# One load for the last values, wo's last piece cut 5/2/1, two issues and two copies moved, in a gated decode step

## The chip, the cores and the metric

One NeuronCore of a Trainium2 chip runs the whole program. The metric is the time of one execution on the device in microseconds (us), as the median of several runs. The profile is one further execution, recorded by the hardware profiler. Its engines: PE (TensorE, matrix multiply), PEld (TensorE's weight loads), DVE (VectorE), ACT (ScalarE), POOL (GpSimd) and SP (SyncE, which here only issues DMAs). "q" behind an engine's name (SPq, PEq) is its sequencer.

## What is computed

Attention of one new token over a cache, and a feed-forward block, mixed by a gate. B = 2 sequences, D = 640, 32 heads of 128, 4096 cached keys and values for each head and sequence, F = 1728, all float32:

```python
q = (x @ wq).reshape(B, 1, 32, 128).transpose(0, 2, 1, 3)
p = softmax(einsum("bhqd,bhkd->bhqk", q, k_cache) * 128**-0.5)
o = einsum("bhqk,bhkd->bhqd", p, v_cache)
a = o.transpose(0, 2, 1, 3).reshape(B, 1, 4096) @ wo
b = silu(x @ w1) @ w2
g = sigmoid((x * gate_w).sum(-1, keepdims=True))
out = g * a + (1 - g) * b
```

The caches are 268 MB of the 298 MB that one execution reads.

## The kernel before

The 64 pairs of head and sequence are taken in 16 items of four heads of one sequence (`items`, N = 16). An item needs 8 MB of keys and 8 MB of values. SBUF holds three slabs of 8 MB: `a` and `b` take the keys of even and odd items, `v` takes values. Item 15 is the exception: its keys are in `b`, and its values go to `a`, which is free by then.

For an item i, DVE and POOL multiply the keys with the query in place (`products`), DVE sums them (`scores`) and finds the peak, ACT makes the exponentials `pz` (`weights`), PE multiplies `pz` with the values in 64 matmuls (`values`, line 734), DVE scales and masks the product (`combine`, line 766), PE folds it with one small product (`gather`, line 782, two matmul instructions), and DVE turns the row into the columns of a stationary operand `oP` (`turn`). PE runs items 0 to 14 in a hardware loop. Item 15 is written out behind the loop.

The weights of the output projection, wo, are 32 rows for each partition, 8 rows for each of four groups (`PR` = 8, `NP` = 4). Groups 0 to 2 land in slab `v` when the values of item 14 are used up; group 3 lands in slab `b`. `project(g)` (accumulate at line 558) multiplies `oP[g]` with the 8 rows of a group. Rows of groups 0 to 2 go to the half of a PSUM bank called `early`, 24 rows of four matmul instructions of 320 columns. Rows of group 3 go to the half called `acc`, 8 rows of eight instructions of 160 columns, in four stripes. `merge` joins the two: ACT copies `early` to SBUF (line 571), then PE adds it to `acc` in eight instructions (line 576). The feed-forward product lies in two further stripes of `early`, which ACT copies long before (line 621). At the end DVE copies `acc` (line 865) and SP stores it.

In the kernel before, the values of item 15 come in three loads of a half, a quarter and a quarter of a slab, and `values(15)` is three operations on PE, each waiting for its own load. Group 3 of wo comes in loads of 4, 3 and 1 rows.

The order on an engine is the order in which the program lists its operations. Each operation waits for the writers of what it reads and for the writers and readers of what it writes (`Flow.op`). A tile's name is the unit: both halves of the PSUM bank bear the name `ps_acc`, and for tiles in PSUM a reader also waits for readers on other engines. DMAs issued by SP run in the order of issue, spread over 16 DMA engines.

At the start SP issues wq (8 MB in slab `a`, 2 MB in `v`), w1 and w2, 19 MB in all, and ACT issues x and the gate's weights, 7.5 KB. PE turns x with the identity matrix (line 386), DVE prepares the gate, PE sums it (line 408), and then comes `mm_qr` (line 433) for the queries. The load of the first keys waits for the first 64 matmuls of `mm_qr`, that of the first values for the product with w1 (line 502), that of the second keys for the feed-forward product (line 607).

Of the kernel before, what the change touches and what calls it, by code (L numbers as in the profile page):

```python
# [142 lines left out]
def gated_decode(nc, x, kc, vc, wq, wo, w1, w2, gate, out):  # L143
    P = 128
    B, H, SK, DH = kc.shape
    D = x.shape[2]
# [6 lines left out]
    NG = C // 4  # L153
# [4 lines left out]
    SLAB = C * DH  # L158
# [5 lines left out]
    W2 = D // 2  # L164
    NP = HQ // 2
    PR = 2 * Q
    items = [(hq, b) for hq in range(HQ) for b in range(B)]
    N = len(items)
    LOOPED = N - 1
# [2 lines left out]
    f = Flow(nc)  # L172
    V, S_, T_, G_ = nc.vector, nc.scalar, nc.tensor, nc.gpsimd

    def sb(name, shape, align=32):
        return nc.alloc_sbuf_tensor(name, shape, F32, align_bytes=align)[tuple([slice(None)] * len(shape))]

    def bank(name):
        return nc.alloc_psum_tensor(name, [P, 512], F32)[:, :]
# [3 lines left out]
    slab = {n: sb(f"slab_{n}", [P, SLAB], 512) for n in "abv"}  # L183

    def part(n, *ks):
        return [f"{n}.{k}" for k in (ks or range(8))]
# [12 lines left out]
    pz = sb("pz", [P, NG, 32])  # L199
    g = sb("g", [P, B])  # L200
# [16 lines left out]
    row = sb("row", [64, DH])  # L217
    oP = [sb(f"oP{i}", [P, PR, 32]) for i in range(NP)]
    oE = sb("oE", [64, PR])
    side = sb("side", [P, 2])  # L220
    partial = sb("partial", [P, W2])
# [3 lines left out]
    ps_q, ps_o, ps_v, ps_acc, ps_t, ps_m, ps_0, ps_1 = (bank(f"ps{i}") for i in range(8))  # L225
    oT = ps_m[:64, 256:512].rearrange("p (n r) -> p n r", r=32)
    early, acc = ps_acc[:, :W2], ps_acc[:, W2 : W2 + W]

    h_q, h_e, h_v, h_o = (f.sem(n) for n in ("next_q", "weights", "values", "rows"))
# [6 lines left out]
    HD = D // 2  # L236
    PD = PR * D

# [6 lines left out]
    def run_of(flat, i):  # L245
        hq, b = items[i]
        return flat[b, hq].rearrange("(p c) -> p c", p=P)
# [7 lines left out]
    def load_v(i):  # L255
        src = run_of(vflat, i)
        if i < N - 1:
            v_load[i] = f.dma("SP", slab["v"], src, writes=part("v"), signal=h_v if i < LOOPED else None)
            return
        cuts = (0, SLAB // 2, 3 * SLAB // 4, SLAB)  # L260
        after = f.users(part("a"))
        for k, (c0, c1) in enumerate(zip(cuts, cuts[1:])):
            f.dma("SP", slab["a"][:, c0:c1], src[:, c0:c1], writes=part("a", k), after=after)

    def load_wo(g):

        n, at = ("v", g * PD) if g < NP - 1 else ("b", 0)
        src = wo[g * PR * P : (g + 1) * PR * P, :].rearrange("(p n) d -> p (n d)", n=PR)
        cuts = (0, PD) if g < NP - 2 else (0, PD // 2, PD) if g < NP - 1 else (0, PD // 2, PD - D, PD)
        after = f.users(part(n)) if g in (0, NP - 1) else wo_after  # L270
        for k, (c0, c1) in enumerate(zip(cuts, cuts[1:])):
            f.dma("SP", slab[n][:, at + c0 : at + c1], src[:, c0:c1], writes=part(n, g % (NP - 1) + k), after=after)
        return after
# [3 lines left out]
    wq_rows = wq.rearrange("(p j) n -> p (j n)", j=J)  # L277
    f.dma("SP", slab["a"], wq_rows[:, :SLAB], writes=part("a"))
    xg = slab["v"][: B + 1, XG_AT : XG_AT + D]
    f.dma("ACT", xg[:B], x.rearrange("b s d -> (b s) d"), writes=part("v", 6))  # L280
    f.dma("ACT", xg[B : B + 1], gate[None, :], writes=part("v", 7))
    f.dma("SP", slab["v"][:, :W1_AT], wq_rows[:, SLAB:], writes=part("v", 0))
    f.dma(
        "SP",
# [2 lines left out]
        writes=part("v", 1, 2, 3, 4, 5),  # L287
# [5 lines left out]
        writes=part("b"),  # L293
# [8 lines left out]
        reads=["ident"],  # L302
        writes=["ident"],
# [9 lines left out]
    for q in range(Q):  # L313
# [3 lines left out]
            writes=["fold"] if q == 0 else [f"fold{q}"],  # L317
# [5 lines left out]
        reads=["ident"],  # L323
        writes=["sel"],
# [4 lines left out]
        reads=["ident"],  # L329
        writes=["half"],  # L330
# [9 lines left out]
        reads=["sel"],  # L340
        writes=["pick"],
# [4 lines left out]
        reads=["sel"],  # L346
        writes=["own"],
# [4 lines left out]
        reads=["ident"],  # L352
        writes=["side"],
    )
    for q in range(Q):
# [5 lines left out]
            reads=["ident"],  # L361
            writes=[f"spread{q}"],
# [3 lines left out]
    for e in range(2):  # L366
# [5 lines left out]
            reads=["ident", "join"],  # L372
            writes=["join"],
# [4 lines left out]
            reads=["ident", "join"],  # L378
            writes=["join"],
# [18 lines left out]
    for b in range(B):  # L398
# [3 lines left out]
            reads=["ps_v", "xz"],  # L402
            writes=[f"gx{b}"],
# [5 lines left out]
        reads=["ones", "gp"],  # L409
        writes=["ps_o"],  # L410
# [7 lines left out]
        reads=["g"],  # L418
        writes=["gc"],
# [59 lines left out]
    for u in range(2):  # L479
# [9 lines left out]
            reads=["ident", f"qall{u}0"],  # L489
            writes=[f"ps_{u}"],  # L490
# [26 lines left out]
    for e in range(2):  # L517
# [3 lines left out]
            reads=["ps_v"],  # L521
            writes=[f"spaced{e}"],
# [8 lines left out]
        reads=["he", "gc"],  # L531
        writes=["he"],
    )
    for e in range(2):
# [5 lines left out]
            reads=["he", "turned", "half"],  # L540
            writes=[f"seq{e}"],
        )

    load_v(0)

    count = {"early": 0, "late": 0}
    total_of = {"early": PR * (NP - 1), "late": PR + 1}

# [16 lines left out]
        f.op("PE", fn, reads=lkeys + wkeys, writes=["ps_acc"])  # L567
        count[to] += 1

    def merge():  # L570
        f.op("ACT", lambda: S_.copy(partial[:64], early[:64, :]), reads=["ps_acc"], writes=["partial"])  # L571

        def fn():
            for n in range(G):
                e, c = divmod(n * W, W2)
                last = T_.matmul(  # L576
                    acc[32 * n : 32 * n + HB + 1, :],
                    join[:, e, :],
                    partial[:, c : c + W],
                    start=False,  # L580
                    stop=False,
                )
            return last

        f.op("PE", fn, reads=["partial", "partial2", "partial3", "join"], writes=["ps_acc"])
        count["late"] += 1

    def project(g):
        n, at = ("v", g * PD) if g < NP - 1 else ("b", 0)
        w = slab[n][:, at : at + PD]  # L590
        to = "early" if g < NP - 1 else "late"
        for k in range(PR):
            lhsT = oP[g][:, k, :] if count[to] == 0 else oP[g][:, k, : HB + 1]
            key = g if g < NP - 2 else g % (NP - 1) + (k >= PR // 2) + (g == NP - 1 and k == PR - 1)
            accumulate(lhsT, w[:, k * D : (k + 1) * D], [f"oP{g}{u}{b}" for u in range(2) for b in range(B)], part(n, key), to)
            if count["late"] == 1:
                merge()

    def ffn_out(n):

        def fn():
            for k in range(FH):
                to = 64 + 32 * (k % 2)
                last = T_.matmul(  # L607
                    early[to : to + 2 * B, :],
                    seq[:, k : k + 2, :].rearrange("p k b -> p (k b)"),
                    slab[n][:, k * HD : (k + 1) * HD],  # L610
                    start=(k < 2),
                    stop=(k >= FH - 2),
                )
            return last

        f.op("PE", fn, reads=["seq0", "seq1"] + part(n), writes=["ps_acc"])
        for k in range(2):
            to = 64 + 32 * k
            f.op(
                "ACT",  # L620
                lambda to=to: S_.copy(partial[to : to + 2 * B], early[to : to + 2 * B, :]),
                reads=["ps_acc"],
                writes=[f"partial{2 + k}"],
            )

    ffn_out("b")
    load_k(1)

# [99 lines left out]
    def values(i, by=(), loop=None):  # L728
        v = slab["v" if i < N - 1 else "a"].rearrange("p (g c) -> p g c", g=NG)

        def groups(g0, g1):
            for gr in range(g0, g1):
                q = gr % 4
                last = T_.matmul(  # L734
                    ps_v[32 * q : 32 * q + 32, :],
                    pz[:, gr, :],
                    v[:, gr, :],
                    start=(gr < 4),
                    stop=(gr >= NG - 4),
                )  # L740
            return last

        if i < N - 1:
            f.op(
                "PE",
                lambda *_: groups(0, NG),
                reads=part("v") + ["pz"],
                writes=["ps_v"],
                by=by,
                loop=loop,  # L750
                lower=[(h_v, 16)],
            )
            return
        cuts = (0, NG // 2, 3 * NG // 4, NG)
        for k, (g0, g1) in enumerate(zip(cuts, cuts[1:])):
            f.op(
                "PE",
                lambda g0=g0, g1=g1: groups(g0, g1),
                reads=part("a", k) + ["pz"],
                writes=["ps_v"],  # L760
            )

    def combine(i):
        ops["combine", i] = f.op(
# [64 lines left out]
    for i in range(N + 1):  # L829
        j = i - 1  # L830
        loop = j if 0 <= j < LOOPED else None
# [10 lines left out]
        if 1 <= i < N:  # L842
            load_v(i)
# [8 lines left out]
        if i == N - 1:  # L852
            wo_after = None
            for g_ in range(NP):
                wo_after = load_wo(g_)
# [7 lines left out]
    for g_ in range(NP):  # L863
        project(g_)
# [56 lines left out]
```

## Time and profile before

| | us |
|---|---|
| median of 3 runs | 696.61 (696.37 to 696.76) |
| the profiled execution | 696.48 |
| its span | 695.2 |
| DVE busy | 489.3 |
| POOL busy | 266.1 |
| PE busy | 224.5 |
| ACT busy | 40.7 |

The span is the time from the first to the last recorded instruction; 1.28 us of the execution lie around it. Busy time is an average over stages, so the tables of shares don't say what sets the end. For that one reads the DMA queues, then the chain that ended last, and then PE's own timeline behind its loop, where the order of its queue can be seen. The granted clock (PEclk) is given as a share of the full 2.4 GHz: 0.50 is 1.2 GHz.

### The profile page before, as it was taken

What the parts mean: (1) busy time and instruction counts of PE and PEld (TensorE: products, weight loads), DVE (VectorE), ACT (ScalarE), POOL (GpSimd) and SP (SyncE); (2) the same over time, 40 slices, a digit from 0 to 9 for tenths busy, and PEclk for the clock granted to TensorE, in tenths of its full rate; (3) what the DMA queues carried; (4) which work ended last, traced back from release to release, by engine and by line L of the source; (5) the groups of instructions that cost most, each with busy time, mean ns of one, the idle gap of its engine ahead of it and who ended that gap; (6) DMA issues with size and microseconds to landing.
All of it is one profiled execution on the core that took longest, in us unless ns stands there. A gap on an engine that the chain in (4) does not pass through costs nothing. (4 is left out here: it accounts for less than half of the span.)

```text
span 695.2 us, 3655 instructions
## 1 busy us (share of the span) xinstructions
PE 224.5 (32%) x1478; PEld 74.7 (11%) x1478; DVE 489.3 (70%) x261; ACT 40.7 (6%) x154; POOL 266.1 (38%) x29
## 2 busy tenths in 40 slices
PE   1653032151331406060412406060503214050678
PEld 1111010010110102020100101010101101010123
DVE  2010958898989597886959595986959595977820
ACT  0000010101010101010010101010000101010100
POOL 1000908191826090815335180906244270907100
PEclk9987556565565757575665757575755757575699
DMA  9999999999999999999999999999999999999997
GB/s 419 406 424 464 422 423 426 426 468 422 426 426 426 468 426 426 426 426 468 426 426 426 426 464 430 423 426 430 464 430 422 426 430 464 430 422 426 420 429 308
DMA packets 6506, 298.37 MB, mean 429 GB/s; under 512 B 727, under 2 KB 735, under 8 KB 994
## 3 DMA queue, kind: packets, MB, share of 16 engines
q1 hardware_dynamic: 6492, 298.26, 99.2%
q8 instruction: 4, 0.07, 0.0%
q14 instruction: 4, 0.03, 0.0%
q10 hardware_dynamic: 6, 0.01, 0.0%
HBM read 298.26 MB, written 0.01 MB: 429 GB/s over the span
## 5 line engine op out<-in xcount | busy, mean ns | idle before, releaser
L734 PE MATMUL ps<-slab_v,pz 128*32 128x512 f32 x960 | 139.2, 745 | 335.4 <-PEq L129 335.4
L638 POOL TENSOR_TENSOR slab_a<-slab_a,qsb 128x7680 f32<-128x7680 f32 x8 | 131.5, 16444 | 207.6 <-DMA slab_a<-in_A_k_cache_dram 192.6
L638 POOL TENSOR_TENSOR slab_b<-slab_b,qsb 128x7680 f32<-128x7680 f32 x8 | 131.5, 16432 | 171.1 <-DMA slab_b<-in_A_k_cache_dram 155.2
L654 DVE TENSOR_REDUCE s<-slab_a 128x68 f32<-128x8704 f32 (+1 forms) x16 | 138.2, 8677 | 0.0
L654 DVE TENSOR_REDUCE s<-slab_b 128x68 f32<-128x8704 f32 (+1 forms) x16 | 138.2, 8676 | 0.0
L644 DVE TENSOR_TENSOR slab_a<-slab_a,ps 128x8704 f32<-128x8704 f32 x8 | 73.7, 9219 | 52.1 <-DMA slab_a<-in_A_k_cache_dram 52.1
L644 DVE TENSOR_TENSOR slab_b<-slab_b,ps 128x8704 f32<-128x8704 f32 x8 | 73.7, 9218 | 47.4 <-DMA slab_b<-in_A_k_cache_dram 47.4
L734 PEld LDWEIGHTS ps<-slab_v,pz 128*32 128x32 f32 x960 | 37.8, 133 | 424.4 <-issue 424.3
L683 ACT ACTIVATE pz<-s,nb 32x128 f32<-32x128 f32 x64 | 25.5, 398 | 559.2 <-PE ps L734 327.2
L782 PE MATMUL ps<-osb,pick 128*128 128x512 f32 x32 | 20.4, 724 | 59.9 <-PEq L129 58.9
L796 DVE TENSOR_REDUCE row<-ps 64x128 f32<-64x512 f32 x16 | 10.9, 682 | 23.3 <-PE ps L782 23.3
L766 DVE SCALAR_TENSOR_TENSOR osb<-ps,rg,own 128x512 f32<-128x512 f32 x16 | 12.0, 749 | 16.7 <-PE ps L734 16.7
L520 DVE COPY spaced<-ps 128x224 f32<-128x224 f32 x2 | 0.7, 387 | 29.9 <-PE ps L502 29.9
L453 PE MATMUL ps<-qall,spread 128*128 (+1 forms) x32 | 7.4, 319 | 37.5 <-PEq L129 36.8
L558 PE MATMUL ps<-slab_v,oP 128*17 128x320 f32 (+1 forms) x96 | 14.9, 475 | 2.1 <-DMA slab_v<-in_A_wo_dram 2.1
L865 DVE COPY ot<-ps 128x160 f32<-128x160 f32 x1 | 0.3, 325 | 19.1 <-PE ps L558 19.1
L782 PEld LDWEIGHTS ps<-osb,pick 128*128 128x128 f32 x32 | 5.4, 211 | 74.0 <-issue 72.1
L453 PEld LDWEIGHTS ps<-qall,spread 128*128 128x128 f32 x32 | 6.8, 224 | 47.6 <-issue 46.0
L683 ACT ACTIVATION_READ_ACCUMULATOR pz<-s,nb 32x1 f32 x64 | 11.8, 184 | 0.0
L433 PE MATMUL ps<-slab_a,xz 128*32 128x512 f32 x64 | 8.4, 687 | 8.6 <-DMA slab_a<-in_A_wq_dram 8.6
L607 PE MATMUL ps<-slab_b,seq 128*4 128x320 f32 x54 | 9.3, 501 | 4.8 <-DMA slab_b<-in_B_w_dram 4.8
L803 DVE STREAM_TRANSPOSE ps<-row 64x256 f32<-64x256 f32 x16 | 10.3, 643 | 0.6
(70 smaller groups left out, 101.5 us busy)
## 6 DMA issues: line engine op xcount, KB each, us to landing
slab_v<-in_A_wo_dram SPq DMA_DIRECT2D x2, 2560.0 KB, 18.5
slab_v<-in_B_w_dram SPq DMA_DIRECT2D x1, 4320.0 KB, 37.8
slab_b<-in_B_w_dram SPq DMA_DIRECT2D x1, 4320.0 KB, 47.4
slab_a<-in_A_v_cache_dram SPq DMA_DIRECT2D x1, 4096.0 KB, 39.3
slab_a<-in_A_v_cache_dram SPq DMA_DIRECT2D x2, 2048.0 KB, 45.9
slab_v<-in_A_wo_dram SPq DMA_DIRECT2D x2, 1280.0 KB, 25.2
slab_v<-in_A_wq_dram SPq DMA_DIRECT2D x1, 2048.0 KB, 26.5
slab_b<-in_A_wo_dram SPq DMA_DIRECT2D x1, 1280.0 KB, 29.1
```

The costliest lines, as they stand in the source:

```text
L453: return T_.matmul(ps_q[:, :DH], spread, qall.rearrange("p h b d -> p (h b) d")[:, i, :], start=True, stop=True,)
L558: last = T_.matmul(dst[32 * n : 32 * n + m, :], lhsT, w[:, n * width : (n + 1) * width], start=first, stop=final,)
L607: last = T_.matmul(early[to : to + 2 * B, :], seq[:, k : k + 2, :].rearrange("p k b -> p (k b)"), slab[n][:, k * HD : (k + 1) * HD], start ...
L638: lambda: G_.tensor_mul(k[:, CV:, :], k[:, CV:, :], qsb[:, None, :].to_broadcast([P, C - CV, DH])),
L644: lambda: V.tensor_mul(k[:, :CV, :], k[:, :CV, :], ps_q[:, None, :DH].to_broadcast([P, CV, DH])),
L654: lambda c0=c0, c1=c1: V.reduce_sum(Ss[i % 2][:, c0:c1], k[:, c0:c1, :], axis=AX.X),
L683: last = S_.activation(pz[lo:hi, :, 4 * q : 4 * q + 4], s[lo:hi].rearrange("p (g c) -> p g c", c=4), AF.Exp, bias=nb[lo:hi], scale=SCALE, ...
L734: last = T_.matmul(ps_v[32 * q : 32 * q + 32, :], pz[:, gr, :], v[:, gr, :], start=(gr < 4), stop=(gr >= NG - 4),)
L766: lambda: V.scalar_tensor_tensor(osb, ps_v.rearrange("p (c d) -> p c d", d=DH), rg, own[:, :, None].to_broadcast([P, 4, DH]), op0=ALU.mult ...
L782: lambda *_: T_.matmul(ps_o, pick, osb.rearrange("p c d -> p (c d)"), start=True, stop=True),
L796: lambda: V.reduce_sum(row, ps_o[:64].rearrange("p (c d) -> p d c", d=DH), axis=AX.X),
L803: lambda: V.transpose(oT.rearrange("p n (e i) -> p n e i", e=2), twice),
```

## The change

- The values of item 15 land as one load of 8 MB, and `values(15)` is one operation of 64 matmuls that waits for it.
- The loads of group 3 of wo have 5, 2 and 1 rows in place of 4, 3 and 1.
- The copy of `early` (ACT) stands directly behind the last row of group 2, and no longer in `merge`; the join stands behind row 5 of group 3 and no longer behind row 1.
- x and the gate's weights are issued by SP, behind the first load of wq, and no longer by ACT.
- The two copies of the feed-forward product go from ACT to DVE.

```diff
+    FIRST = 5
@@ load_v
-        cuts = (0, SLAB // 2, 3 * SLAB // 4, SLAB)
-        after = f.users(part("a"))
-        for k, (c0, c1) in enumerate(zip(cuts, cuts[1:])):
-            f.dma("SP", slab["a"][:, c0:c1], src[:, c0:c1], writes=part("a", k), after=after)
+        f.dma("SP", slab["a"], src, writes=part("a"))
@@ load_wo
-        cuts = (0, PD) if g < NP - 2 else (0, PD // 2, PD) if g < NP - 1 else (0, PD // 2, PD - D, PD)
+        cuts = (0, PD) if g < NP - 2 else (0, PD // 2, PD) if g < NP - 1 else (0, FIRST * D, PD - D, PD)
@@
-    f.dma("ACT", xg[:B], x.rearrange("b s d -> (b s) d"), writes=part("v", 6))
-    f.dma("ACT", xg[B : B + 1], gate[None, :], writes=part("v", 7))
+    f.dma("SP", xg[:B], x.rearrange("b s d -> (b s) d"), writes=part("v", 6))
+    f.dma("SP", xg[B : B + 1], gate[None, :], writes=part("v", 7))
@@
+    def copy_early():
+        f.op("ACT", lambda: S_.copy(partial[:64], early[:64, :]), reads=["ps_acc"], writes=["partial"])
+
     def merge():
-        f.op("ACT", lambda: S_.copy(partial[:64], early[:64, :]), reads=["ps_acc"], writes=["partial"])
...
@@ project
-            key = g if g < NP - 2 else g % (NP - 1) + (k >= PR // 2) + (g == NP - 1 and k == PR - 1)
+            key = g if g < NP - 2 else g + (k >= PR // 2) if g < NP - 1 else (k >= FIRST) + (k == PR - 1)
             accumulate(lhsT, w[:, k * D : (k + 1) * D], [f"oP{g}{u}{b}" for u in range(2) for b in range(B)], part(n, key), to)
-            if count["late"] == 1:
+            if to == "early" and count[to] == total_of[to]:
+                copy_early()
+            if count["late"] == FIRST:
                 merge()
@@ ffn_out
-                "ACT",
-                lambda to=to: S_.copy(partial[to : to + 2 * B], early[to : to + 2 * B, :]),
+                "DVE",
+                lambda to=to: V.tensor_copy(partial[to : to + 2 * B], early[to : to + 2 * B, :]),
@@ values
-        cuts = (0, NG // 2, 3 * NG // 4, NG)
-        for k, (g0, g1) in enumerate(zip(cuts, cuts[1:])):
-            f.op(
-                "PE",
-                lambda g0=g0, g1=g1: groups(g0, g1),
-                reads=part("a", k) + ["pz"],
-                writes=["ps_v"],
-            )
+        f.op(
+            "PE",
+            groups,
+            reads=part("v" if i < N - 1 else "a") + ["pz"],
+            writes=["ps_v"],
...
```

## Rows read from the trace of the kernel before

**Rows 1.** The page's DMA queues: queue, packets, MB, share of 16 engines.

```profile
q1 hardware_dynamic: 6492, 298.26, 99.2%
```

**Rows 2.** The chain that ended last: start us, us, what.

```profile
660.01 29.10 DMA slab_b<-in_A_wo_dram
...
689.25 0.51 PE ps L558 x8
...
689.78 0.43 ACT partial L571
...
690.25 0.47 PE ps L576 x8
690.72 2.06 PE ps L558 x56
```

**Rows 3.** Timeline of PE, 656 to 696: start us, us, engine, line, operation [idle before].

```profile
660.33 0.38 PE L708 MATMUL ps<-rs,fold 128*128 128x1 f32 x2
660.64 5.36 PE L734 MATMUL ps<-slab_a,pz 128*32 128x512 f32 x48
667.80 1.92 PE L734 MATMUL ps<-slab_a,pz 128*32 128x512 f32 x16 [1.80 <-DMA slab_a<-in_A_v_cache_dram]
670.67 1.13 PE L782 MATMUL ps<-osb,pick 128*128 128x512 f32 x2 [0.94 <-DVE osb L766]
673.92 14.85 PE L558 MATMUL ps<-slab_v,oP 128*32 128x320 f32 x96 [2.13 <-DMA slab_v<-in_A_wo_dram]
```

**Rows 4.** DMA issues (last line: from 619.1 to 619.5): KB each, us to landing.

```profile
slab_b<-in_B_w_dram SPq DMA_DIRECT2D x1, 4320.0 KB, 47.4
slab_a<-in_A_v_cache_dram SPq DMA_DIRECT2D x1, 4096.0 KB, 39.3
slab_a<-in_A_v_cache_dram SPq DMA_DIRECT2D x2, 2048.0 KB, 45.9
slab_b<-in_A_wo_dram SPq DMA_DIRECT2D x1, 320.0 KB, 31.2
...
slab_a<-in_A_v_cache_dram SPq DMA_DIRECT2D x1, 2048.0 KB, 43.7
```

**Rows 5.** Stretches of PE: from:to us, PE busy us (instructions), granted clock, DMA share, GB/s.

```profile
618.34:622.98 4.64, 1.66 (x6) 1.00 1.04 452
622.98:630.00 7.02, 0.00 (x0) 0.50 1.03 448
674.18:677.59 3.41, 3.41 (x16) 0.50 0.93 402
680.00:688.00 8.00, 8.00 (x62) 1.00 1.01 427
```

**Rows 6.** Timeline of PE, the longest and shortest `values` of the loop's fifteen.

```profile
378.03 10.04 PE L734 MATMUL ps<-slab_v,pz 128*32 128x512 f32 x64 [27.11 <-PEq L129]
...
493.99 8.38 PE L734 MATMUL ps<-slab_v,pz 128*32 128x512 f32 x64 [27.08 <-PEq L129]
```

**Rows 7.** Timeline of PE's weight loads, 656 to 696: the wait ahead of wo's group 1.

```profile
679.98 0.12 PEld L558 LDWEIGHTS ps<-slab_v,oP 128*17 128x17 f32 x4 [0.47 <-DMA slab_v<-in_A_wo_dram]
```

**Rows 8.** Timeline of the first 60 us: PE, and SP's issue of the first keys.

```profile
10.47 2.36 PE L386 MATMUL ps<-ident,slab_v 3*128 3x3 f32 x10 [10.47 <-DMA slab_v<-in_gate_w_dram]
13.63 0.59 PE L408 MATMUL ps<-gp,ones 128*128 128x2 f32 x2 [0.80 <-DVE gp L405]
22.87 8.43 PE L433 MATMUL ps<-slab_a,xz 128*32 128x512 f32 x64 [8.64 <-DMA slab_a<-in_A_wq_dram]
...
31.36 0.33 SPq L68 DMA_DIRECT2D slab_a<-in_A_k_cache_dram  x1
...
39.44 5.43 PE L502 MATMUL ps<-slab_v,xz 128*32 128x432 f32 x40 [3.51 <-DMA slab_v<-in_B_w_dram]
```

**Rows 9.** Timeline of ACT and DVE, 59 to 72: the copies, and DVE's next operation.

```profile
59.04 0.85 ACT L621 COPY partial<-ps 4x320 f32<-4x320 f32 x2 [12.46 <-PE ps L607]
68.91 9.22 DVE L644 TENSOR_TENSOR slab_a<-slab_a,ps 128x8704 f32<-128x8704 f32 x1 [21.10 <-DMA slab_a<-in_A_k_cache_dram]
```

More of the change, by code (lines that the diff above doesn't have):

```diff
@@ L729, in values, with groups @@
         v = slab["v" if i < N - 1 else "a"].rearrange("p (g c) -> p g c", g=NG)
-        def groups(g0, g1):
-            for gr in range(g0, g1):
+        def groups(*_):
+            for gr in range(NG):
                 q = gr % 4
@@ L741, in groups @@
             return last
-        if i < N - 1:
-            f.op(
-                "PE",
-                lambda *_: groups(0, NG),
-                reads=part("v") + ["pz"],
-                writes=["ps_v"],
-                by=by,
-                loop=loop,
-                lower=[(h_v, 16)],
-            )
-            return
-        cuts = (0, NG // 2, 3 * NG // 4, NG)
-        for k, (g0, g1) in enumerate(zip(cuts, cuts[1:])):
-            f.op(
-                "PE",
-                lambda g0=g0, g1=g1: groups(g0, g1),
-                reads=part("a", k) + ["pz"],
-                writes=["ps_v"],
-            )
+        f.op(
[3 more added lines that the diff above has]
+            writes=["ps_v"],
+            by=by,
+            loop=loop,
+            lower=[(h_v, 16)],
+        )
     def combine(i):
```

## The prediction, made before the change was run

> **What bounds the kernel now.** I read the DMA queues first. SP's queue moves 298.26 MB and keeps the 16 DMA engines busy for 99.2% of the span [rows 1]. So nothing that runs beside the stream counts, as long as the next load is issued before the one ahead of it has landed. What counts is the tail: what is left to do when the last bytes land. Second, the chain of waits. Its last long piece is the landing of wo's group 3, 29.10 us after an issue at 660.01, so at 689.11. Then follow the first row of group 3, ACT's copy (689.78, 0.43), the join (690.25) and 56 matmuls that end at 692.78 [rows 2]. The load of the last row is issued two steps of 0.47 us after 660.01 and takes 31.2 us [rows 4]: it lands near 692.15, only 0.63 before PE's end. The tail of before is thus bound by the landing, and PE keeps up with it. Third, PE's own order behind its loop, because the change moves work there: the sum of the weights at 660.33, 48 matmuls of the last values at 660.64, a wait of 1.80, the other 16 at 667.80, gather at 670.67, and from 673.92 the 96 matmuls of wo's groups 0 to 2, which end at 688.77, 0.34 before group 3 lands [rows 2, 3]. That 0.34 us is all the room PE has. Fourth, the clock: the 96 matmuls include 3.41 us at 0.50 (1.2 GHz) [rows 5].
>
> **One load for the last values.** Bytes and order in SP's queue stay, so I let the stream run as before. The pieces land 39.3 and 43.7 us after their issues, and the third 2 x 45.9 - 43.7 = 48.1 [rows 4]. With issues 0.47 apart the second and third piece land 4.9 us after one another, and 2048 KB in 4.9 us is 430 GB/s: no gap between pieces that one load could close. The whole load then lands where the third piece does, and PE starts at 667.80 [rows 3]. What is new: none of the 64 matmuls can run before that. The 48 that lay at 660.64, beside the transfer, come behind 667.80. Behind `values(15)` on PE's queue stand gather, all of `project` and the join, so all of PE's tail moves.
>
> How long do the 64 take? Between 660.7 and 667.8 PE has nothing to do. In the loop PE works 1.66 us between 618.34 and 622.98, behind a pass's values, and from 622.98 on the clock is 0.50 while PE idles [rows 5]. A gap of 7.1 us holds less work than these 4.64 us, so I take the 64 to begin at 1.2 GHz, like those of the loop, which follow an idle stretch too. The loop's fifteen take 8.38 to 10.04 us [rows 6]; the middle is 9.21. At the upper clock the same 64 take 5.36 + 1.92 = 7.28 [rows 3]. So `values(15)` ends at 676.18 to 677.84, middle 677.01.
>
> The rest of PE's queue, one after the other:
> - To the end of gather: before, 669.72 to 671.80, 2.08 us [rows 3] (combine on DVE and gather), and 0.04 for the next start.
> - Groups 0 to 2 of wo, 96 matmuls: 14.85 before [rows 3]. Of this 3.41 us ran at the half clock [rows 5], which costs 1.70, and some 0.3 was a wait for group 1 [rows 7]. That leaves 12.85. The bounds are 13.15 (no wait taken off) and 12.4 (62 instructions in 8.00 us at full clock [rows 5], times 96). Their data has landed by then, so nothing is hidden any more. PE was busy on the values just before, with only some 0.95 us of pause, so I take the full clock.
> - ACT's copy. It now stands directly behind the last row of group 2, which is meant to put it beside the landing of group 3. But the rows of group 3 write the same tile name that the copy reads, so by the order of the program the first of them waits for the copy. The handover is 689.76 to 690.25, 0.49 us [rows 2]. Before, it lay behind row 1; now it lies ahead of row 1. It is free only if PE is done early, and PE is not.
> - Group 3 and the join: 64 + 8 = 72 matmuls of 160 columns. 56 took 2.06 [rows 2], so 72 take 2.65; the upper bound is 72/64 of 2.53 (690.25 to 692.78), 2.85.
>
> Sum: 677.01 + 2.08 + 0.04 + 12.85 + 0.49 + 2.65 = 695.12. PE ended at 692.78, so the end moves by +2.34 us; from +1.5 to +3.2 for the spread of the values alone, and +1.05 to +3.7 with the bounds of the other terms. On the profiled execution (696.48) that gives 698.8, on the median, 0.13 above it, 698.95. I say 698.9.
>
> A page bears on that spread. The fifteen passes differ by up to 1.66 us with the same work [rows 6], so the rise falls differently against the start of each. The Trainium skill, "TensorE: Matmul & The Clock Gate", "What's actually happening", says that the activity monitor runs freely and does not start anew with a kernel. By that rule executions of one kernel would differ among themselves by up to 0.83 us to either side of the sum; if the rise were tied to the program, all would share one value of the spread. One trace cannot show which.
>
> **wo in 5, 2 and 1 rows.** Bytes and last piece stay, so it lands near 692.15. With PE late, every piece has landed when its rows come up: cost and gain 0. With PE early, the end would be that landing plus the 0.63 of before, so there is no gain either way. Moving the join behind row 5 only orders the same 72 matmuls.
>
> **x and gate on SP.** They stand behind the first part of wq in SP's queue. On ACT's queue the gate's row let PE start at 10.47 [rows 8]. In the trace nothing small is queued on SP behind a large load, so the bounds are 10.47 and the landing of wq's first part, 22.87 [rows 8]; I take the later. Then PE's turn of x, the gate and its sum (10.47 to 14.22, 3.75 us) come ahead of `mm_qr`, which starts near 26.6 and not at 22.87. The first keys' issue moves from 31.36 to some 35 (37 if more of it runs at the lower clock). The queue has work until w2 lands, 47.4 us after an issue near 2.2, at 49.6 [rows 4]: over 12 us of cover. The product with w1 moves from 39.44 to 43 at most, and the loads behind it wait on a queue that is full for 20 us more. The two issues push the next issues of SP by under 1 us while 8 MB are on their way. Cost 0; without that cover it would be 3.75 us.
>
> **Two copies on DVE.** 0.85 us on ACT at 59.04; DVE waits for keys until 68.91 [rows 9]. At the same price they end at 60, with 9 us of cover. Cost 0, up to 0.85 without it.
>
> **The rivals.**
> - PE keeps up (not slower). If the clock stays at its upper level through the gap, the 64 matmuls take 7.28 and the sum is 695.12 - 1.93 = 693.19, +0.41, so 697.0: no change. The deciding point is the clock at 667.8: at 1.00 this holds, at 0.50 the forecast. For it: between 666.0 and 673.92 PE worked only 1.92 + 1.13 us [rows 3] and the clock fell no earlier than 674.18. Against it: the fall at 622.98, and that even the shortest pass of the loop is longer than the 7.28 us [rows 3, 6]. Chance 0.08.
> - The clock falls again in the pause around gather. Before, such a stretch of 3.41 us followed the wait of 2.13 at 673.92 [rows 3, 5] and cost 1.70; here the wait for wo is gone and the pause is half as long. It would give 700.6. Chance 0.06.
> - Fewer loads shorten the stream (faster). The rows show pieces that land back to back, and two loads fewer would then save nothing. If each load had a price of its own in the stream, up to the 0.47 by which SP's issues stand apart, two fewer would save 0.9 and the tail as before would give 695.7; but only if PE kept up as well. Chance 0.03. The Trainium skill, "DMA: Bandwidth & Descriptors", "Anatomy of one DMA — SWDGE (gpsimd) path", fits 2.0 us of fixed time for each DMA of another issuing path; by that figure two loads less would be worth 4 us, and the trace, with pieces landing back to back, does not agree for loads queued behind one another.
>
> **How the numbers follow.** The forecast, PE bound by the whole of `values(15)` behind the landing, has the remaining 0.83. Its time is 698.1 to 699.8 by the clock alone, 697.7 to 700.3 with the bounds. I give 697.6 to 700.4; outside lie most of the third rival, half of the first and of the second. A measurement of this kernel tells about 0.2%, 1.4 us, from no change, so slower means above 698.0. The forecast's low end, 0.05, lies below that and goes to "same" with the first rival: slower 0.84, same 0.13, faster 0.03.
>
> **What would show it.** In the changed kernel's timeline: one group of 64 matmuls of line 734's successor from 667.8 to about 677, the first microseconds at 0.50; no wait for wo ahead of or within the 96 matmuls; the 96 ending near 692 and not at 688.8; ACT's copy right behind; the last 72 without a wait for a DMA; the last landing still near 692.15; the first keys issued near 35 with no gap in the stream. I am wrong if the 96 still end before group 3 lands, if the landing of the last values moves by more than half a microsecond, or if the stream has a gap at 49 us.

## The result, and the profile after

| | before | changed |
|---|---|---|
| median of 8 runs, us | 696.74 (696.37 to 697.10) | 698.95 (698.26 to 699.45) |
| the profiled execution, us | 696.48 | 698.32 |
| its span, us | 695.2 | 696.9 |

The changed kernel takes 1.0030 times as long, 95% interval 1.0019 to 1.0041: 2.2 us more. 698.9 was forecast, in a range of 697.6 to 700.4. The profiled execution is one of the shorter of the eight, which matters below.

The chain that ended last in the changed kernel (start us, us, what; x64 means 64 instructions) shows the whole mechanism. It answers to [rows 2]:

```profile
618.81 48.82 DMA slab_a<-in_A_v_cache_dram
667.63 0.04 issue
667.67 8.72 PE ps L735 x64
...
676.49 0.76 DVE osb L757
...
677.29 1.12 PE ps L773 x2
678.42 13.04 PE ps L556 x96
691.46 0.57 issue
692.03 1.56 PE ps L556 x40
693.59 0.27 PE ps L575 x8
693.86 0.85 PE ps L556 x24
```

Before, the last long piece was the landing of wo's group 3, and PE had 0.63 us of work behind the last row's landing. Now the chain leaves the stream at the landing of the last values, 667.63, and from there on runs through PE to the end: 64 matmuls, gather, 96 matmuls, a pause of 0.57, 72 matmuls. No DMA stands in it any more. PE ends at 694.71 and not at 692.78.

The stream itself is what it was. DMA issues of the changed kernel (KB, us to landing; the view gives no KB for the load of 8 MB), beside [rows 4]:

```profile
slab_b<-in_A_wo_dram SPq DMA_DIRECT2D x1, 320.0 KB, 31.0
...
slab_a<-in_A_v_cache_dram SPq DMA_DIRECT2D x1, 48.8
```

The load of the last values lands where the third piece did (667.63, against PE's start at 667.80 in [rows 3]), and wo's last row 31.0 us after its issue, where it took 31.2. One load of 8 MB is not faster here than its three pieces.

Stretches of PE in the changed kernel (from:to, PE busy us and instructions, granted clock, DMA share, GB/s), beside [rows 5]:

```profile
662.00:664.10 2.10, 0.00 (x0) 1.00 1.15 499
664.10:667.63 3.53, 0.00 (x0) 0.50 0.68 294
667.67:670.93 3.26, 3.26 (x16) 0.50 0.98 421
670.93:676.39 5.46, 5.41 (x52) 1.00 1.02 439
678.42:691.46 13.04, 13.04 (x96) 1.00 0.93 389
```

Where the 48 matmuls of [rows 3] lay, PE now idles. The clock falls to 1.2 GHz at 664.10, and the 64 matmuls run their first 3.26 us at that level. The 96 matmuls of wo then have the full clock and no wait.

### The profile page after: what moved, and what is told of

Same layout as the page of the kernel before. It is cut to its first block, busy times and chain, and to the rows that moved or that the text cites. A ratio compares the mean times of both kernels' runs of the same rounds, so it can differ in the third digit from the quotient of the medians.

```text
span 696.9 us, 3653 instructions
## 1 busy us (share of the span) xinstructions
PE 220.6 (32%) x1478; PEld 74.5 (11%) x1478; DVE 490.2 (70%) x263; ACT 40.0 (6%) x152; POOL 266.2 (38%) x29
## 5 line engine op out<-in xcount | busy, mean ns | idle before, releaser
L735 PE MATMUL ps<-slab_v,pz 128*32 128x512 f32 x960 | 136.1, 730 | 337.8 <-PEq L129 337.8
L556 PE MATMUL ps<-slab_v,oP 128*17 128x320 f32 (+1 forms) x96 | 13.1, 433 | 0.0
L735 PE MATMUL ps<-slab_a,pz 128*32 128x512 f32 x64 | 8.7, 702 | 6.9 <-DMA slab_a<-in_A_v_cache_dram 6.9
```

The costliest lines, as they stand in the source:

```text
L556: last = T_.matmul(dst[32 * n : 32 * n + m, :], lhsT, w[:, n * width : (n + 1) * width], start=first, stop=final,)
L735: last = T_.matmul(ps_v[32 * q : 32 * q + 32, :], pz[:, gr, :], v[:, gr, :], start=(gr < 4), stop=(gr >= NG - 4),)
```

## Experiments

Each kernel was run beside the kernel before on one chip. The kernel before had medians of 696.67 to 696.88 beside the experiments and 696.74 beside the changed kernel, so a difference of medians between two experiments is uncertain by some 0.2 us more than their spread shows. Where products are added, their result is not used.

**One part alone: the last values in one load.**

```diff
 (the kernel before)
-        cuts = (0, SLAB // 2, 3 * SLAB // 4, SLAB)
...
+        f.dma("SP", slab["a"], src, writes=part("a"))
... and values(15) in one operation
```

> The kernel before with one part of the change alone: the last values land as one load and values(15) is one operation. Everything else as before. Theory (PE has its whole remaining queue behind that one landing, and the low clock and the copy add to it): all of the loss comes with this part, 698.9 (698.1 to 699.7), and 0.2 more than in the changed kernel at most, since row 1 of group 3 now drains ahead of the copy. In the timeline 64 matmuls from 667.7, no wait for a DMA behind them, 96 matmuls ending near 692. Rival (the cost sits in wo's 5, 2, 1 rows, in the place of ACT's copy, or in x and the gate on SP's queue): within 0.3 us of the kernel before, 696.7.

Measured: 699.58 (698.74 to 699.78, 5 runs), 1.0040 times before (1.0026 to 1.0054). The end of its chain:

```profile
678.45 13.37 PE ps L555 x96
...
691.84 0.43 ACT partial L568
...
692.32 0.47 PE ps L573 x8
692.78 1.95 PE ps L555 x56
```

PE ends at 694.73, as in the changed kernel (694.71). So this one part brings the whole loss, and the place of the copy makes no difference to PE's end when PE is late: ahead of group 3 or behind its first row, PE waits for it. The median lies 0.6 above the changed kernel's, more than the 0.2 expected. The two profiled executions (698.74 and 698.32) differ by 0.4, and that lies behind PE: the span ends 2.6 us after PE's end here (span 697.3) and 2.2 in the changed kernel. With five runs of a kernel whose executions differ by 1 us, the rest is not settled. One load and one operation came together here; three loads with one operation were not run.

**All parts but that one.**

```diff
 (the changed kernel)
-        f.dma("SP", slab["a"], src, writes=part("a"))
+        cuts = (0, SLAB // 2, 3 * SLAB // 4, SLAB)
+        after = f.users(part("a"))
+        for k, (c0, c1) in enumerate(zip(cuts, cuts[1:])):
+            f.dma("SP", slab["a"][:, c0:c1], src[:, c0:c1], writes=part("a", k), after=after)
... and values(15) in three operations, as before
```

> The changed kernel with its other parts (wo in 5, 2, 1 rows, the copy ahead of group 3, x and gate on SP, two copies on DVE), but the last values in three loads and three operations as before. Theory: the other parts cost and bring nothing, 696.7 (696.4 to 697.1); the 96 matmuls end before 689.3, the copy lies beside the landing of group 3, the last landing is near 692.0 and PE ends 0.6 to 0.7 behind it. Rival (the parts bring something that the late values hide): below 696.2. Rival (they carry part of the loss): above 697.3.

Measured: 696.38 (696.22 to 696.85, 11 runs), 0.9994 (0.9985 to 1.0003). PE's timeline, and ACT's copy:

```profile
668.27 2.81 PE L738 MATMUL ps<-slab_a,pz 128*32 128x512 f32 x16 [2.82 <-DMA slab_a<-in_A_v_cache_dram]
...
674.39 5.27 PE L559 MATMUL ps<-slab_v,oP 128*32 128x320 f32 x32 [0.32 <-DMA slab_v<-in_A_wo_dram]
680.45 8.80 PE L559 MATMUL ps<-slab_v,oP 128*17 128x320 f32 x64 [0.79 <-DMA slab_v<-in_A_wo_dram]
690.48 1.56 PE L559 MATMUL ps<-slab_b,oP 128*32 128x160 f32 x40 [1.23 <-DMA slab_b<-in_A_wo_dram]
...
689.30 0.42 ACT L572 COPY partial<-ps 64x320 f32<-64x320 f32 x1 [29.57 <-PE ps L559]
```

PE waits for wo three times. The copy (689.30 to 689.72) lies beside the landing of group 3, as the change means it to, and PE starts group 3 only when a DMA lets it. The other parts cost nothing that the measurement shows.

**Does the clock carry part of the loss?** Extra work keeps PE busy in the gap.

```diff
 (the changed kernel, between total(15) and values(15))
+        if i == N - 1:
+
+            def keep():
+                for _ in range(7):
+                    last = T_.matmul(qr[0], spread, qall[:, :HALF, 0, :], start=True, stop=True)
+                return last
+
+            f.op("PE", keep, reads=SPREAD + ["qall00"], writes=["ps_0"])
```

> The changed kernel with seven extra products of 128x512 on PE (14 instructions, their result is not used) between the sum of the weights at 660.4 and values(15). They need nothing that lands late and are done, at some 0.85 us each, near 666.5, ahead of the landing at 667.7. Theory (part of the loss is the low clock at which the 64 matmuls start): the granted clock is 1.00 from 660 to the end, the 64 take 7.3 us and not 8.4 to 10.0, and the time falls by 1.0 to 2.4 us to 697.1 (696.7 to 697.7), although PE does 6 us more. Rival (the delay is in PE's queue alone and the clock plays no part): 698.9 or more.

Measured: 696.85 (11 runs, ten of them 696.68 to 697.27, one 698.81, which stays unexplained), 1.0004 (0.9995 to 1.0013). Timeline of PE, and the stretch of the 64:

```profile
660.32 6.25 PE L748 MATMUL ps<-qall,spread 128*128 128x512 f32 x14
667.72 7.07 PE L735 MATMUL ps<-slab_a,pz 128*32 128x512 f32 x64 [1.15 <-DMA slab_a<-in_A_v_cache_dram]
...
676.79 13.11 PE L556 MATMUL ps<-slab_v,oP 128*32 128x320 f32 x96
690.47 1.56 PE L556 MATMUL ps<-slab_b,oP 128*32 128x160 f32 x40 [0.57 <-ACT partial L569]
```

```profile
667.72:674.80 7.08, 7.07 (x64) 1.00 1.02 437
```

```profile
692.31 0.85 PE ps L556 x24
```

6.25 us more work on PE make the kernel 2.1 us shorter. The 64 take 7.07 at the full clock, and the time is that of the kernel before. PE ends at 693.16 (the last line, from the chain). This is the first rival of the prediction, made true by hand: 693.19 for PE and 697.0 for the time were its price.

**The copy's wait.**

```diff
 (the changed kernel; the sums of group 3 in another PSUM bank)
-    early, acc = ps_acc[:, :W2], ps_acc[:, W2 : W2 + W]
+    early, acc = ps_acc[:, :W2], ps_1[:, :W]
...
-        f.op("PE", fn, reads=lkeys + wkeys, writes=["ps_acc"])
+        f.op("PE", fn, reads=lkeys + wkeys, writes=["ps_acc" if to == "early" else "ps_1"])
... the join and the last copy use "ps_1" likewise
```

> The changed kernel with the sums of group 3 in another PSUM bank (the one of the queries, free by then), so that the first row of group 3 no longer waits for ACT's copy of the early sums; the join still does, behind row 5. Theory (PE is the bound and the copy's handover of 0.49 us lies on its path): 0.4 to 0.6 us less, 698.4, and no pause in PE between the 96 matmuls and group 3. Rival (a landing is the bound there and hides the copy): 698.9, the pause moves to a wait for a DMA.

Measured: 698.34 (697.61 to 699.20, 11 runs), 1.0023 (1.0014 to 1.0032): 0.6 below the changed kernel's median. Its chain and ACT's copy:

```profile
678.63 14.27 PE ps L556 x132
```

```profile
691.72 0.42 ACT L569 COPY partial<-ps 64x320 f32<-64x320 f32 x1 [31.19 <-PE ps L556]
```

PE goes from the 96 matmuls into group 3 without a pause (132 in one piece are the 96 and the first 36 of group 3), and the copy lies beside PE's work. The pause came from the order that the program gives to one tile name, which this edit splits in two. The intervals of the two kernels overlap, so that the 0.5 of this term rests on the missing pause in the trace as much as on the medians.

**Extra work of a known size, with one load.**

```diff
 (the changed kernel, between gather(15) and project(0))
+    def extra():
+        for _ in range(2):
+            last = T_.matmul(qr[0], spread, qall[:, :HALF, 0, :], start=True, stop=True)
+        return last
+
+    f.op("PE", extra, reads=SPREAD + ["qall00"], writes=["ps_0"])
```

> The changed kernel with two extra products of 128x512 (4 instructions, their result is not used) on PE between gather of item 15 and the first row of wo. Fourteen such instructions took 6.25 us where the clock was kept up, so four take 1.7 to 1.8. Theory (PE alone sets the end behind the landing of the last values): the time rises by all of it, to 700.6 (700.2 to 701.3). Rival (a landing or the copy sets the end and leaves room): less than 0.8 us more.

Measured: 701.02 (700.22 to 701.34, 4 runs), 1.0058 (1.0042 to 1.0075). PE's timeline and the stretch at the low clock:

```profile
668.01 9.56 PE L735 MATMUL ps<-slab_a,pz 128*32 128x512 f32 x64 [7.73 <-DMA slab_a<-in_A_v_cache_dram]
...
679.48 1.88 PE L856 MATMUL ps<-qall,spread 128*128 128x512 f32 x4
681.29 13.11 PE L556 MATMUL ps<-slab_v,oP 128*32 128x320 f32 x96
```

```profile
668.01:673.07 5.06, 5.06 (x24) 0.50 0.99 425
```

The extra work takes 1.81 us to the start of the 96, and the median is 2.07 above the changed kernel's: all of it reaches the end. In this execution the 64 ran 5.06 us at the low clock and took 9.56, where the changed kernel's profile has 3.26 and 8.66, although the two programs are the same up to there.

**The same extra work with three loads.** The edit is the same, in the kernel of all parts but one.

> The same 1.7 to 1.8 us of extra work at the same place, but with the last values in three loads (all other parts of the change in). Theory: with three loads PE waits 2.3 us in all for wo in this stretch (0.32, 0.79 and 1.23 in its profile), so the extra work fits into the waits and the time stays within 0.5 us of the kernel before, 696.7; if the clock falls low in the wait ahead of wo, up to 0.5 more. Rival (PE has only the 0.34 us of room that stands between the 96 matmuls and the landing in the trace of before): 1.3 to 1.5 more, 698.1.

Measured: 696.39 (696.19 to 696.76, 10 runs), 0.9994 (0.9985 to 1.0004).

```profile
672.06 1.88 PE L869 MATMUL ps<-qall,spread 128*128 128x512 f32 x4
674.32 4.50 PE L559 MATMUL ps<-slab_v,oP 128*32 128x320 f32 x32 [0.39 <-DMA slab_v<-in_A_wo_dram]
680.38 8.80 PE L559 MATMUL ps<-slab_v,oP 128*17 128x320 f32 x64 [1.56 <-DMA slab_v<-in_A_wo_dram]
690.40 1.56 PE L559 MATMUL ps<-slab_b,oP 128*32 128x160 f32 x40 [1.22 <-DMA slab_b<-in_A_wo_dram]
```

The same 1.8 us cost nothing here. They fill the wait ahead of group 0 of wo, and PE still waits 0.39, 1.56 and 1.22. That the wait ahead of group 0 is only 0.32 in the profile without the extra work has another reason: there the granted clock was 0.66 over the last 16 matmuls of the values (668.27 to 671.10) and 0.50 over gather, which together took 1.84 us longer than here (2.81 and 2.08, against 1.93 and 1.12).

**Two halves.**

```diff
 (against the kernel of all parts but one)
-        cuts = (0, SLAB // 2, 3 * SLAB // 4, SLAB)
+        cuts = (0, SLAB // 2, SLAB)
... and values(15) in two operations
```

> The changed kernel with the last values in two halves and two operations of 32 matmuls. Theory: 32 matmuls run beside the transfer, 32 behind 667.7; at the full clock these take 3.6 us, gather is done at 673.4 and PE then waits for wo as in the kernel before, so 696.7; where the clock falls in the pause from 664 to 667.7, up to 3 us more for them, of which the waits for wo take 2 and more: 696.7 to 697.7. Rival (the loss is proportional to the work behind the last landing, 16 matmuls costing 0 and 64 costing 2.1): 697.4.

Measured: 696.35 (696.19 to 696.74, 10 runs), 0.9996 (0.9987 to 1.0006).

```profile
667.57 5.19 PE L738 MATMUL ps<-slab_a,pz 128*32 128x512 f32 x32 [3.40 <-DMA slab_a<-in_A_v_cache_dram]
...
679.77 8.79 PE L559 MATMUL ps<-slab_v,oP 128*17 128x320 f32 x64 [0.51 <-DMA slab_v<-in_A_wo_dram]
689.73 1.57 PE L559 MATMUL ps<-slab_b,oP 128*32 128x160 f32 x40 [1.16 <-DMA slab_b<-in_A_wo_dram]
```

```profile
667.33:670.74 3.41, 3.17 (x16) 0.50 0.92 396
```

Even here the clock is low for most of the first 3.4 us behind the landing and the second half takes 5.19, 1.6 more than the first (3.64 at full clock). PE's waits for wo take all of it. The loss is therefore not proportional to the work behind the last landing, which would have given 697.4: it sets in where the room is used up, between 32 and 64 matmuls.

**Both repairs.** Extra work in the gap and the other PSUM bank.

> The changed kernel with both repairs: the seven products that keep the clock up ahead of the last values, and the sums of group 3 in another PSUM bank, so that nothing waits for the copy but the join. Theory (the two terms are separate and PE is the bound until the last landing): 0.5 less than with the clock kept alone as long as PE ends later than 0.6 behind the last landing at 692.0; PE would end near 692.65 and the time is 696.3. Rival (with the clock kept a landing is the bound already): 696.85, as with the clock kept alone.

Measured: 696.41 (10 runs, nine of them 696.21 to 696.85, one 697.82, which stays unexplained), 0.9999 (0.9989 to 1.0009). PE, the end of the chain, and ACT:

```profile
689.89 1.56 PE L556 MATMUL ps<-slab_b,oP 128*32 128x160 f32 x40
```

```profile
691.73 0.91 PE ps L556 x24
```

```profile
689.97 0.42 ACT L569 COPY partial<-ps 64x320 f32<-64x320 f32 x1 [29.43 <-PE ps L556]
```

0.44 below the clock kept alone, and the intervals overlap; but PE ends at 692.64 and not at 693.16, 0.52 earlier, without a wait for the copy. With both repairs, one load costs no more than three. But it brings nothing over them either. So of the later end of PE in the changed kernel (694.71 against 692.78) some 1.55 us are the clock (694.71 against 693.16) and some 0.5 the copy.

**Do the other parts bring something?** The kernels without the one load lie 0.35 to 0.5 below the kernel before that ran beside them. Two more runs were to tell where that comes from: wo and the copy alone, and x and the gate alone.

> The kernel before with wo's group 3 in 5, 2 and 1 rows, the copy of the early sums directly behind group 2 and the join behind row 5; the last values in three loads, x and gate on ACT's queue, the small copies on ACT. The runs with all parts but the one load lie at 696.4, 0.35 to 0.5 below the kernel before, which is more than the 0 of the prediction. Theory A (it comes from the tail: with 3 + 1 rows before, PE still has four rows to go when the second piece lands at 691.4, and with 2 + 1 only three): 0.2 to 0.4 less than before, and PE ends 0.55 to 0.65 behind the last landing. Theory B (it comes from the queue of x and gate): as before.

> The kernel before with x and gate issued by SP and nothing else. Theory of the prediction: no change, the first keys issued near 35 to 37 and no gap in the stream. Theory B (the small transfers on a second queue cost the stream something at the start): 0.3 less than before. If its chain is late: a gap in the stream at 49 us and 0.5 or more above.

Measured: 696.52 (696.16 to 696.99) and 696.48 (696.09 to 696.83), 11 runs each, both 0.9997 (0.9988 to 1.0006), beside 696.67 of before. The two differ from before by 0.15 and 0.19 us, inside the interval, and not from one another. Neither theory is shown; whether there are 0.2 us in these parts stays open, and it is less than a measurement of this kernel can tell. One stretch of the traces points at x and the gate: from PE's end to the end of the span it takes 2.4 to 2.6 us in the three profiles with these two issues on ACT's queue (before, the last values alone, wo and the copy alone) and 2.1 to 2.2 in the nine with them on SP's. Of before's longer stretch, though, most does not reach the time of the execution: that lies 3.70 behind PE's end before and 3.64 with x and the gate alone. No kernel here beats the one before by more than those 0.5 us.

## Why the prediction was right

**The bound.** The forecast hung on 0.34 us between the end of the 96 matmuls and the landing of group 3 [rows 2, 3]. The pair with the same extra work shows it directly: with one load all of 1.8 us reaches the end, with three loads none. The 0.34 was too narrow a reading of the room, though: with three loads PE also waits ahead of groups 0 and 1, and 1.8 us vanished in those waits. For the forecast this did not matter, because the one load moved PE by more than all of them: in the changed kernel no wait for wo is left ahead of the 96 or within them.

**The terms**, of the changed kernel's profiled execution:

| step | forecast | measured |
|---|---|---|
| start of the 64 | 667.80 | 667.67 |
| the 64 matmuls | 8.38 to 10.04, middle 9.21 | 8.72 |
| to the first of the 96 | 2.12 | 2.03 |
| the 96 | 12.85 (12.4 to 13.15) | 13.04 |
| the copy's handover | 0.49 | 0.57 |
| group 3 and the join | 2.65 (up to 2.85) | 2.68 |
| end of PE | 695.12 | 694.71 |

No term is off by more than 0.2 but the 64, whose place in the spread no single trace could give. Of the 0.3 that the forecast took off the 96 for a wait [rows 7], little was there: without it they stand at 13.15, nearer to the 13.04. The sum over the execution shown is +1.93 at PE's end, the median of eight +2.2. That the median came within 0.05 us of the forecast is partly luck: the 64 alone could have moved it by 0.83 to either side.

**The clock.** The forecast let the 64 begin at 1.2 GHz, since in the loop the clock stands at that level while PE idles [rows 5]. It fell at 664.10 with PE idle, and the first 3.26 us ran at the low level. With the clock kept up the loss is gone, at the price that the first rival named.

The Trainium skill, "TensorE: Matmul & The Clock Gate", "What's actually happening", says that the activity monitor runs freely and does not start anew with a kernel. The traces agree, without proving it: in the two kernels that are the same up to this point the rise comes 3.26 and 5.06 us behind the start of the 64. In the four kernels with one load and nothing in the gap, the 64 took 8.60, 8.66, 8.90 and 9.56. The changed kernel's eight executions spread over 1.19 us, while ten of eleven with the clock kept spread over 0.59 (the eleventh lies 1.5 above them).

**The other rivals.** The clock did not fall again around gather: the 96 ran at 1.00 throughout. Fewer loads did not shorten the stream: the one load landed at 667.63, and PE took up the third piece at 667.80. The Trainium skill, "DMA: Bandwidth & Descriptors", "Anatomy of one DMA — SWDGE (gpsimd) path", gives a fixed 2.0 us for each DMA of another issuing path. With 0.17 us between one load and three pieces, the traces show no such price for loads queued behind one another here.

**x and the gate.** Rows of PE, SP and the DMAs' rate from the first 60 us of the changed kernel, beside [rows 8]:

```profile
22.92 2.36 PE L384 MATMUL ps<-ident,slab_v 3*128 3x3 f32 x10 [22.92 <-DMA slab_v<-in_gate_w_dram]
...
26.61 10.04 PE L431 MATMUL ps<-slab_a,xz 128*32 128x512 f32 x64
...
41.22 3.83 PE L500 MATMUL ps<-slab_v,xz 128*32 128x432 f32 x40
```

```profile
36.72 0.33 SPq L68 DMA_DIRECT2D slab_a<-in_A_k_cache_dram  x1
```

```profile
45.00:50.00 5.00, 0.51 (x8) 0.97 1.21 525
50.00:55.00 5.00, 5.00 (x29) 0.69 1.03 446
```

The small loads land behind wq's first part, at the upper of the two bounds. `mm_qr` starts at 26.61 (26.6 forecast), the first keys are issued at 36.72 (35 to 37), and the stream has no gap around 49.6, where w2 lands.

**The copies on DVE** took 1.00 and not 0.85, with DVE idle until 68.73:

```profile
58.97 1.00 DVE L622 COPY partial<-ps 4x320 f32<-4x320 f32 x2 [10.98 <-PE ps L608]
68.73 9.22 DVE L645 TENSOR_TENSOR slab_a<-slab_a,ps 128x8704 f32<-128x8704 f32 x1 [8.77 <-DMA slab_a<-in_A_k_cache_dram]
```

## What to carry to other kernels

Here the stream of loads bounded the kernel, and its tail was decided by how much of one engine's in-order queue had to wait for a late landing, not by the number of loads. In such a kernel, sum up everything that stands behind the landing in that queue, and compare it with what is left of the stream and with all of the engine's waits on the way, not with the last one alone. Cut the last load only as fine as that room asks (two halves did here what three pieces did). Look up the granted clock behind an idle gap: behind gaps of 3.40 and 6.92 us the burst began at 0.50 here. Check whether a copy meant to be hidden is ordered ahead of its successor by a shared tile name, as that of the PSUM bank here.

## What the runs showed of the hardware

More work made an engine faster here: with 6.25 us of unused products ahead of the landing, the 64 matmuls behind it took 7.07 us at a granted clock of 1.00, and 8.66 without them, of which the first 3.26 us ran at 0.50. And the last landing of the full stream is not a fixed moment. In the kernel with all parts but one, wo's last row took 32.2 us from its issue, which comes two steps of 0.47 after the issue of group 3's first piece; the chain and the DMA issues there:

```profile
659.45 30.89 DMA slab_b<-in_A_wo_dram
```

```profile
slab_b<-in_A_wo_dram SPq DMA_DIRECT2D x1, 320.0 KB, 32.2
```

That is a landing at 692.6, where the kernel before had 692.15 with the same bytes, and this execution (696.80) was at the upper end of its runs. What made it late is not shown.
